# Threshold attention and mixer: weights transposed SBUF to SBUF, value product turned over, mixer in small pieces

## The chip, the cores and the metric

The kernel runs on one core of a Trainium2 chip. The metric is the device time of one execution in microseconds. Inputs and output lie in DRAM as float32.

## What is computed

Eight batches, eight heads, 576 positions, head size 64. Attention keeps only scores within tau = 0.02 of each row's maximum; the heads, laid side by side, form x (576 x 512), which goes through a mixer: a low-rank product over positions (rank 32), then a two-layer network over channels (512 to 2048 to 512), both with a residual.

```python
scores = scale * np.matmul(q, k.transpose(0, 1, 3, 2))
thresh = np.max(scores, axis=-1, keepdims=True) - tau
scores = np.where(scores >= thresh, scores, -1000000000.0)
attn = np.exp(scores - np.max(scores, axis=-1, keepdims=True))
attn = attn / (np.sum(attn, axis=-1, keepdims=True) + 1e-09)
x = np.matmul(attn, v)          # then the heads side by side: (B, 576, 512)
u = x + (x.transpose(0, 2, 1) @ U @ V).transpose(0, 2, 1)
out = u + np.maximum(u @ w_ch1, 0.0) @ w_ch2
```

## The kernel before

Work goes by pairs of heads: 32 pairs, four to a batch. For each pair:

- **Loads** (L104, L105, L111, L114, on POOL's queue): q and k in tiles of 96 rows, v in tiles of 128.
- **Transposes** (L132, L135, on PE): 12 transposes of 96 rows give q and k with both heads' 64 features on 128 partitions; ACT copies them out of PSUM and scales q by 1/8.
- **Scores** (L152): five row tiles (four of 128 rows, one of 64), per head a float32 product with 64 contracted rows, in two column halves of 288. A float32 matmul stands as two records in the trace, so a pair has 5 x 2 x 2 x 2 = 40. A score tile takes two PSUM banks; two such buffers exist.
- **Row work**, per head and row tile: DVE copies the scores out and takes the row maximum in one pass (L155), then the negated maximum (L166) and the threshold (L168); ACT takes the exponential (L171); DVE masks it, `(s >= thr) * e`, in bfloat16 (L178). That last step is put off by one tile (`deferred`).
- **Weights transposed**: SP writes each masked tile to a scratch in DRAM (L181), whose rows are padded from 576 to 640 columns by a fill (L306, on POOL); after a head's last tile, one transposing DMA (L184) brings all 576 rows back as `wt_sb`, keys on the partitions.
- **Value product** (L202), issued two pairs later: v is split into a bfloat16 part and a bfloat16 remainder with a column of ones between (L116 to L123), and for each of five row tiles and five key tiles the transposed weights are the stationary side and the 130 columns of v move: 50 matmuls a pair. ACT copies the result (L210), DVE adds the two parts (L211) and the ones column gives the denominator.

After a batch's fourth pair the mixer is queued as four stages, one run in each of the next pairs' turns: `mixer_m1` (division L218 to L223, cast L230, low-rank products L233 and L239), `mixer_m2` (transposes L253), `mixer_m3` (first layer, 128 matmuls L266, relu on ACT L273), `mixer_m4` (second layer, 80 matmuls L282, residual L285, output DMA). The last batch's stages run alone at the end. A scheduler puts the instructions of each engine in order; every engine then runs its own list in that order.

Of the kernel before, what the change touches and what calls it, by code (L numbers as in the profile page):

```python
# [12 lines left out]
ALU = mybir.AluOpType  # L13

# [4 lines left out]
NB96 = S // 96  # L19
QTILES = [(0, 128), (128, 128), (256, 128), (384, 128), (512, 64)]  # L20
KTILES = QTILES
SCHUNK = 288
WSCR_COLS = 640

DEBUG_X = False
# [3 lines left out]
def kernel(  # L29
# [16 lines left out]
    consts = ctx.enter_context(tc.tile_pool(name="consts", bufs=1))  # L46
    ident_f = consts.tile([P, P], FP32, name="ident_f")
    make_identity(nc, ident_f)
    zpad = consts.tile([96, NB96, WSCR_COLS - S], BF16, name="zpad")
    nc.vector.memset(zpad, 0.0)  # L50

    wpool = ctx.enter_context(tc.tile_pool(name="weights", bufs=1))
    W1b = wpool.tile([P, 4, F], BF16, name="W1b")
    W2b = wpool.tile([P, 16, DM], BF16, name="W2b")
    Ub = wpool.tile([P, 5, R], BF16, name="Ub")
    Vb = wpool.tile([R, S], BF16, name="Vb")

    xpool = ctx.enter_context(tc.tile_pool(name="xpool", bufs=2))

    rawpool = ctx.enter_context(tc.tile_pool(name="raw", bufs=2))  # L60
    vrawpool = ctx.enter_context(tc.tile_pool(name="vraw", bufs=4))
    vaugpool = ctx.enter_context(tc.tile_pool(name="vaug", bufs=4))
    qkTpool = ctx.enter_context(tc.tile_pool(name="qkT", bufs=4))
    sbpool = ctx.enter_context(tc.tile_pool(name="ssb", bufs=3))
    smallpool = ctx.enter_context(tc.tile_pool(name="small", bufs=24))
    avpool = ctx.enter_context(tc.tile_pool(name="avpool", bufs=4))
    epool = ctx.enter_context(tc.tile_pool(name="epool", bufs=3))
    wrowpool = ctx.enter_context(tc.tile_pool(name="wrows", bufs=6))
    wtpool = ctx.enter_context(tc.tile_pool(name="wtpool", bufs=4))
    mpool = ctx.enter_context(tc.tile_pool(name="mix", bufs=2))  # L70
    m1pool = ctx.enter_context(tc.tile_pool(name="mix1", bufs=1))
    opool = ctx.enter_context(tc.tile_pool(name="opool", bufs=3))
    dpool = ctx.enter_context(tc.tile_pool(name="wscr", bufs=8, space=bass.MemoryType.DRAM))
    psc = ctx.enter_context(tc.tile_pool(name="psc", bufs=2, space=bass.MemoryType.PSUM))
    pav = ctx.enter_context(tc.tile_pool(name="pav", bufs=2, space=bass.MemoryType.PSUM))
    psm = ctx.enter_context(tc.tile_pool(name="psm", bufs=2, space=bass.MemoryType.PSUM))

    with tc.tile_pool(name="wstage", bufs=2) as st:
        su = st.tile([P, 5, R], FP32, name="us_", tag="us_")
        nc.gpsimd.dma_start(su[:, 0:4, :], moe_U[0:4 * P, :].rearrange("(t p) r -> p t r", p=P))  # L80
        nc.gpsimd.dma_start(su[0:64, 4, :], moe_U[4 * P:S, :])
        nc.vector.tensor_copy(out=Ub[:, 0:4, :], in_=su[:, 0:4, :])
        nc.vector.tensor_copy(out=Ub[0:64, 4, :], in_=su[0:64, 4, :])
        sv = st.tile([R, S], FP32, name="vs_", tag="vs_")
        nc.gpsimd.dma_start(sv, moe_V[:, :])
        nc.vector.tensor_copy(out=Vb, in_=sv)
        for t in range(4):
            for qt in range(4):
                s1 = st.tile([P, F // 4], FP32, name="w1s", tag="stage_big")
                nc.gpsimd.dma_start(  # L90
                    s1, moe_w_ch1[t * P:(t + 1) * P, qt * (F // 4):(qt + 1) * (F // 4)]
                )
                nc.vector.tensor_copy(out=W1b[:, t, qt * (F // 4):(qt + 1) * (F // 4)],
                                      in_=s1)
        for c in range(16):
            s2 = st.tile([P, DM], FP32, name="w2s", tag="stage_big")
            nc.gpsimd.dma_start(s2, moe_w_ch2[c * P:(c + 1) * P, :])
            nc.vector.tensor_copy(out=W2b[:, c, :], in_=s2)

    def emit_raw_qk(b, hp):  # L100
        qpair = rawpool.tile([96, NB96, 2, D], FP32, name="qpair", tag="qpair")
        kpair = rawpool.tile([96, NB96, 2, D], FP32, name="kpair", tag="kpair")
        for j, h in enumerate((2 * hp, 2 * hp + 1)):
            nc.gpsimd.dma_start(qpair[:, :, j, :], q[b, h].rearrange("(t p) d -> p t d", p=96))  # L104
            nc.gpsimd.dma_start(kpair[:, :, j, :], k[b, h].rearrange("(t p) d -> p t d", p=96))  # L105
        return qpair, kpair

    def emit_v_build(b, hp):
        vraw = vrawpool.tile([P, 5, 2, D], FP32, name="vraw", tag="vraw")
        for j, h in enumerate((2 * hp, 2 * hp + 1)):  # L110
            nc.gpsimd.dma_start(  # L111
                vraw[:, 0:4, j, :], v[b, h][0:4 * P, :].rearrange("(t p) d -> p t d", p=P)
            )
            nc.gpsimd.dma_start(vraw[0:64, 4, j, :], v[b, h][4 * P:S, :])  # L114
# [30 lines left out]
    def emit_scores_and_w(b, hp, qTpk, kTpk, wscrs, strips_out, deferred):  # L145
        for i, (qs, nq) in enumerate(QTILES):
            for j in (0, 1):
# [40 lines left out]
                if deferred:  # L188
                    deferred.pop(0)()
# [137 lines left out]
    if n_pairs > 1:  # L327
        raw_tiles[1] = emit_raw_qk(*pairs[1])
# [82 lines left out]
```

## Time and profile before

| | us |
|---|---|
| median of 3 runs | 1102.98 |
| lowest and highest run | 1101.51, 1124.68 |
| span of the profiled execution, first to last instruction | 1099.2 |
| PE busy (matmuls) | 999.8 |
| DVE busy | 718.9 |
| ACT busy | 484.5 |
| POOL busy | 245.7 |

The profiled execution's own time is known by its span; the median of the runs lies 3.8 us above it. The page has one row for each group of like instructions: line, engine, operation, tiles written and read, count, then busy time and mean length, then the idle time of the engine ahead of them and what ended it. Busy time of a group counts overlapping instructions once, so on PE, where matmuls overlap, busy time over count is less than the mean length.

### The profile page before, as it was taken

The page shows a single profiled execution, that of the slowest core. Times are in us where ns is not written, and L with a number is a line of the kernel's source. Part 1 is how long each engine was busy: PE and PEld are TensorE (multiplying, and loading weights), DVE is VectorE, ACT ScalarE, POOL GpSimd, SP SyncE. Part 2 cuts the span into 40 slices and gives each one's busy share as a digit, 9 for nine tenths or more (in the row PEclk, how much of TensorE's full clock was granted, in tenths as well). Part 3 has the DMA queues.
Part 4 walks back from the last instruction along what each step waited for, and adds up shares of the span by engine and source line. Part 5 has one row for each costly group of instructions (what it writes and reads, how often), then busy time and mean ns, then how long its engine had stood idle before and what let it go on. Part 6 is the DMA issues. An engine that isn't in the chain of part 4 may idle for free.

```text
span 1099.2 us, 16099 instructions
## 1 busy us (share of the span) xinstructions
PE 999.8 (91%) x5168; PEld 558.7 (51%) x5168; DVE 718.9 (65%) x2396; ACT 484.5 (44%) x1089; POOL 245.7 (22%) x363
## 2 busy tenths in 40 slices
PE   4886877999999998999998998999999999999898
PEld 3443443565545654555544655555545555456444
DVE  4864676866768558766677568675587666785521
ACT  2332341573436633554325634456335644366141
POOL 6544576412112220312112211122203011000000
PEclk9999965899959997889958998699968999599969
DMA  5789787575335563565546663366534543343401
GB/s 168 210 227 164 173 186 149 137 160 140 114 93 155 135 153 98 115 139 118 148 102 134 116 163 100 95 138 138 152 97 128 132 116 114 84 119 92 114 0 44
DMA packets 252725, 141.73 MB, mean 129 GB/s; under 512 B 197808, under 2 KB 238784, under 8 KB 252640
## 3 DMA queue, kind: packets, MB, share of 16 engines
q1 hardware_dynamic: 233600, 99.12, 38.6%
q0 software_dynamic: 19040, 41.59, 14.7%
q8 instruction: 40, 0.66, 0.3%
q14 instruction: 45, 0.37, 0.1%
HBM read 36.85 MB, written 56.62 MB: 85 GB/s over the span
## 4 chain that ended last, share of the span: by engine, by line
PE 75%; DMA 12%; DVE 7%; issue 4%; ACT 2%; SPq 0%; POOL 0%; DVEq 0%; POOLq 0%; ACTq 0%
PE sc L152 24%; PE avps L202 14%; PE p1ps L266 13%; PE chps L282 13%; DMA wt_sb<-wscr 10%; PE qkTps L132 4%; PE utps L253 3%; PE ttps L233 2%; PE hps L239 2%; DVE s_sb L155 2%; DVE xun L223 2%; DMA wscr<-w_sb 1%; DVE w_sb L178 1%; PE qkTps L135 1%; SPq L184 0%
## 5 line engine op out<-in xcount | busy, mean ns | idle before, releaser
L152 PE MATMUL sc<-qkTpk 64*128 64x288 f32 (+1 forms) x1280 | 393.3, 514 | 16.9 <-DVE s_sb L155 16.4
L155 DVE TENSOR_SCALAR_CACHE_REDUCE s_sb<-sc 128x576 f32<-128x576 f32 (+1 forms) x320 | 237.9, 748 | 157.4 <-PE sc L152 155.9
L171 ACT ACTIVATE e_sb<-s_sb,negm 128x576 bf16<-128x576 f32 (+1 forms) x320 | 246.3, 775 | 176.8 <-DVE thr L168 99.4
L178 DVE SCALAR_TENSOR_TENSOR w_sb<-s_sb,thr,e_sb 128x576 bf16<-128x576 f32 (+1 forms) x320 | 258.9, 809 | 22.4 <-ACT e_sb L171 21.7
L152 PEld LDWEIGHTS sc<-qkTpk 64*128 64x128 f32 (+1 forms) x1280 | 207.5, 212 | 106.4 <-DVE s_sb L155 39.0
L202 PE MATMUL avps<-vaug,wt_sb 128*128 128x130 bf16 (+3 forms) x1600 | 212.9, 250 | 42.5 <-DMA wt_sb<-wscr 35.4
L202 PEld LDWEIGHTS <-wt_sb 128*128 128x128 bf16 (+3 forms) x1600 | 125.5, 107 | 201.2 <-issue 107.1
L266 PE MATMUL p1ps<-uT,W1b 128*128 128x288 bf16 x1024 | 157.0, 292 | 0.7
L210 ACT COPY avsb<-avps 128x130 f32<-128x130 f32 (+1 forms) x320 | 79.3, 266 | 167.0 <-PE avps L202 154.9
L282 PE MATMUL chps<-W2b,Rb 128*128 128x512 bf16 (+1 forms) x640 | 146.5, 380 | 0.0
L104 POOL DMA_DIRECT2D qpair<-in_q_dram x64 | 47.4, 741 | 394.0 <-PE qkTps L135 334.7
L273 ACT ACTIVATE Rb<-p1ps 128x288 bf16<-128x288 f32 x256 | 104.4, 410 | 58.4 <-PE p1ps L266 50.8
L266 PEld LDWEIGHTS <-W1b 128*128 128x128 bf16 x1024 | 95.8, 99 | 55.1 <-issue 29.6
L285 DVE TENSOR_TENSOR o_sb<-chps,u_f 128x512 f32<-128x512 f32 (+1 forms) x40 | 27.5, 688 | 105.9 <-PE chps L282 105.9
L282 PEld LDWEIGHTS <-Rb 128*128 128x128 bf16 (+1 forms) x640 | 60.6, 100 | 69.4 <-issue 3.6
L111 POOL DMA_DIRECT2D vraw<-in_v_dram x64 | 49.4, 771 | 199.5 <-DVE xun L211 101.9
L137 ACT ACTIVATE qkTpk<-qkTps 128x480 f32<-128x480 f32 x32 | 18.2, 570 | 132.3 <-PE qkTps L132 127.6
L211 DVE TENSOR_TENSOR xun<-avsb 128x65 f32<-128x65 f32 (+1 forms) x320 | 59.1, 216 | 24.2 <-ACT avsb L210 22.2
L105 POOL DMA_DIRECT2D kpair<-in_k_dram x64 | 47.6, 744 | 41.1 <-PE qkTps L135 37.8
L306 POOL DMA_DIRECT2D wscr<-zpad x64 | 46.8, 738 | 5.7 <-DMA vraw<-in_v_dram 4.0
L166 DVE TENSOR_SCALAR negm<-mrow 128x1 f32<-128x1 f32 (+1 forms) x320 | 46.2, 144 | 0.5
L168 DVE TENSOR_SCALAR thr<-mrow 128x1 f32<-128x1 f32 (+1 forms) x320 | 44.9, 140 | 0.0
(52 smaller groups left out, 525.3 us busy)
## 6 DMA issues: line engine op xcount, KB each, us to landing
wscr<-w_sb SPq DMA_DIRECT2D x256, 144.0 KB, 1.8
qpair<-in_q_dram POOLq DMA_DIRECT2D x64, 144.0 KB, 3.1
kpair<-in_k_dram POOLq DMA_DIRECT2D x64, 144.0 KB, 3.1
vraw<-in_v_dram POOLq DMA_DIRECT2D x64, 128.0 KB, 4.4
out_dram<-o_sb SPq DMA_DIRECT2D x32, 256.0 KB, 2.3
wscr<-zpad POOLq DMA_DIRECT2D x64, 72.0 KB, 4.7
wscr<-w_sb SPq DMA_DIRECT2D x64, 72.0 KB, 2.0
w1s<-in_moe_w_ch_dram POOLq DMA_DIRECT2D x16, 256.0 KB, 3.4
```

The costliest lines, as they stand in the source:

```text
L105: nc.gpsimd.dma_start(kpair[:, :, j, :], k[b, h].rearrange("(t p) d -> p t d", p=96))
L111: nc.gpsimd.dma_start(vraw[:, 0:4, j, :], v[b, h][0:4 * P, :].rearrange("(t p) d -> p t d", p=P))
L152: nc.tensor.matmul(sct[0:nq, ci, 0:SCHUNK], lq, rk, start=True, stop=True)
L155: nc.vector.tensor_scalar(out=s_sb[0:nq, :].rearrange("p (a c) -> p a c", a=2), in0=sct[0:nq, :, 0:SCHUNK], scalar1=0.0, scalar2=None, op0 ...
L171: nc.scalar.activation(out=e_sb[0:nq, :], in_=s_sb[0:nq, :], func=ACT.Exp, bias=negm[0:nq, :])
L178: nc.vector.scalar_tensor_tensor(out=w_sb[0:nq, :], in0=s_sb[0:nq, :], scalar=thr[0:nq, :], in1=e_sb[0:nq, :], op0=ALU.is_ge, op1=ALU.mult)
L202: nc.tensor.matmul(avps[0:nq, slot, :], wt_sb[0:nk, kt, qs:qs + nq], vaug[0:nk, kt, j, :], start=(kt == 0), stop=(kt == 4),)
L210: nc.scalar.copy(out=avsb[0:nq, :], in_=avps[0:nq, slot, :])
L211: nc.vector.tensor_add(out=xun[0:nq, qc, h, :], in0=avsb[0:nq, 0:D + 1], in1=avsb[0:nq, D + 1:2 * D + 2])
L266: nc.tensor.matmul(p1[:, 0:SCHUNK], W1b[:, dt_, ft * P:(ft + 1) * P], uT[:, dt_, ci * SCHUNK:(ci + 1) * SCHUNK], start=(dt_ == 0), stop=(d ...
L273: nc.scalar.activation(out=Rb[:, ft, ci * SCHUNK:(ci + 1) * SCHUNK], in_=p1[:, 0:SCHUNK], func=ACT.Relu)
L282: nc.tensor.matmul(chps[0:ns, :], Rb[:, ft, ss:ss + ns], W2b[:, ft, :], start=(ft == 0), stop=(ft == 15))
```

## The change

Nearly the whole body is written anew. What is computed stays; these parts differ:

- **Rows are renumbered.** Position p * 9 + t sits on partition p of tile t, so that a load takes runs of up to five rows; tile t holds nine 64-row pieces, two to a 128-row tile, the fifth tile having one. q, k and v take four loads each. U, V and the output follow the same numbering.
- **Transposes of q and k**: four of 128 rows and one of 64, each.
- **Scores**: both heads of a row tile get their buffers together and are issued in turn, column half by column half; the two 64-row tails share one buffer, one head on partitions 0 to 63, the other on 64 to 127. This gives nine row tiles a pair instead of ten. q is scaled by -1/8, so minimum takes the place of maximum and the negated maximum is not needed; one threshold instruction serves both heads.
- **Masking** (`scalar_tensor_tensor`) writes into a ring of eight tiles whose columns 576 to 639 are zero from the start, and also sums its rows, which gives the denominator.
- **Weights transposed** straight from that ring into `wT`, SBUF to SBUF, one DMA for each row tile and head (two for the shared tail), all from SP. The DRAM scratch, its writes and its fills are gone. One small DMA moves the 64 denominators of the tail's second head.
- **Value product turned over**: v (split in two parts as before, the cast on ACT, the remainder on POOL) is stationary, 64 columns for each head in its own half of the array's columns, and 288 columns of `wT` move: 5 x 2 x 2 x 2 = 40 matmuls a pair. The result is transposed back by five PE transposes, and the division is folded into the copy out of PSUM.
- **Mixer** cut into 84 pieces in a queue; after each row tile's scores two pieces of the value product of the pair before and five mixer pieces are issued. It starts after the next batch's first pair.
- **PSUM**: two score buffers (two banks each) as before; everything else shares four one-bank buffers instead of two and two.
- Large weights are cast by their DMA instead of on DVE.

The diff, cut to its core:

```diff
-                sct = psc.tile([P, 2, 512], FP32, name="sc", tag="sc")
-                lq = qTpk[64 * j:64 * j + 64, qs:qs + nq]
-                for ci in range(2):
-                    rk = kTpk[64 * j:64 * j + 64, ci * SCHUNK:(ci + 1) * SCHUNK]
-                    nc.tensor.matmul(sct[0:nq, ci, 0:SCHUNK], lq, rk, start=True, stop=True)
...
-                    nc.sync.dma_start(wscrs[j][qs:qs + nq, 0:S], w_sb[0:nq, :])
-                    if last_row:
-                        strips = wtpool.tile([P, 5, S], BF16, name="wt_sb", tag="wt_sb")
-                        nc.sync.dma_start_transpose(strips[:, :, :],
-                                                    wscrs[j][0:S, 0:WSCR_COLS])
...
+    psS = pool("psS", 2, PSUM)
+    ps1 = pool("ps1", 4, PSUM)
...
+                sct = [psS.tile([P, 2, 512], FP32, name="sc", tag="sc") for _ in range(2)]
+                for c in range(2):
+                    for j in range(2):
+                        hs = slice(64 * j, 64 * j + 64)
+                        nc.tensor.matmul(sct[j][:, c, 0:HC], self.qT[hs, i * P:(i + 1) * P],
+                                         self.kT[hs, c * HC:(c + 1) * HC], start=True, stop=True)
...
+                w_sb = w_ring[ring[0] % NW]
+                ring[0] += 1
+                nc.vector.scalar_tensor_tensor(
+                    out=w_sb[:, 0:S], in0=ssb[x], scalar=thr[:, x:x + 1], in1=esb[x],
+                    op0=ALU.is_le, op1=ALU.mult, accum_out=self.den[:, i, x:x + 1])
+                if i < 4:
+                    nc.sync.dma_start_transpose(self.wT[:, :, x, i * P:(i + 1) * P], w_sb[:, :])
+                else:
+                    for j in range(2):
+                        nc.sync.dma_start_transpose(self.wT[:, :, j, 512:S],
+                                                    w_sb[64 * j:64 * j + 64, :])
+            if i == 4:
+
+                nc.sync.dma_start(self.den[0:HB, 4, 1:2], self.den[HB:P, 4, 0:1])
...
+                for part in range(2):
+                    for c in range(2):
+                        for j in range(2):
+                            nc.tensor.matmul(
+                                st["av"][c][64 * j:64 * j + 64, 0:HC],
+                                self.vh[0:nk, kt, part, j, :],
+                                self.wT[0:nk, kt, j, c * HC:(c + 1) * HC],
+                                start=(kt == 0 and part == 0), stop=(kt == 4 and part == 1))
...
+        for i in range(NT):
+            pair.scores(i)
+            if i == 1 and p + 1 < NP:
+                pairs[p + 1].prepare_qk()
+            if i == 3 and p + 1 < NP:
+                pairs[p + 1].prepare_v()
+            pop(applyq, 2)
+
+            pop(mixq, 5)
+            if i == 1 and p >= 1:
+
+                applyq.extend(pairs[p - 1].apply_units(xs[pairs[p - 1].b]))
```

How the order of instructions moves, at three places.

On PE, in the middle of a pair before. Names are line, operation, tile written <- tiles read, shape; numbers tell buffers apart:

```order
L152 MATMUL sc_5634<-qkTpk_5065,qkTpk_5054 128x288 x2
L152 MATMUL sc_5649<-qkTpk_5065,qkTpk_5054 128x288 x2
L202 LDWEIGHTS wt_sb_5232
L202 MATMUL avps_5730<-vaug_4585,wt_sb_5232 128x130
...
L282 MATMUL chps_5816<-W2b_69,Rb_5338 128x512
...
L152 MATMUL sc_5664<-qkTpk_5065,qkTpk_5054 128x288 x2
```

and now:

```order
L174 MATMUL sc_3949<-qkT_3564,qkT_3554 128x288
L174 MATMUL sc_3950<-qkT_3564,qkT_3554 128x288
...
L322 MATMUL p1_3919<-uT_3522,W1b_66 128x288
...
L174 MATMUL sc_3949<-qkT_3564,qkT_3554 128x288
L174 MATMUL sc_3950<-qkT_3564,qkT_3554 128x288
...
L229 MATMUL av_3970<-wT_3470,vh_3408 64x288
L229 MATMUL av_3970<-wT_3470,vh_3408 64x288
```

The two heads now alternate; here the scheduler has also put five mixer pieces (20 matmuls) between the two column halves of one score group.

On DVE, one row tile before:

```order
L155 TENSOR_SCALAR s_sb_5160,mrow_5161<-sc_5157 128x576
L178 SCALAR_TENSOR_TENSOR w_sb_5154<-s_sb_5145,thr_5149,e_sb_5152 128x576
L166 TENSOR_SCALAR negm_5163<-mrow_5161 128x1
L168 TENSOR_SCALAR thr_5164<-mrow_5161 128x1
L155 TENSOR_SCALAR s_sb_5175,mrow_5176<-sc_5172 128x576
```

and now:

```order
L190 TENSOR_SCALAR s_sb_4254,m_4252<-sc_4246 128x576
L190 TENSOR_SCALAR s_sb_4256,m_4252<-sc_4247 128x576
L200 TENSOR_SCALAR thr_4253<-m_4252 128x2
L205 SCALAR_TENSOR_TENSOR w_ring3_73,den_4130<-s_sb_4254,thr_4253,e_sb_4258 128x576
L205 SCALAR_TENSOR_TENSOR w_ring4_74,den_4130<-s_sb_4256,thr_4253,e_sb_4260 128x576
```

Both reductions of a row tile now stand ahead of both maskings, with one threshold between.

On SP, about one pair before:

```order
L181 DMA wscr<-w_sb 128x576 x6
L181 DMA wscr<-w_sb 64x576
L184 DMA_TRANSPOSE wt_sb<-wscr 128x5x576
L181 DMA wscr<-w_sb 64x576
L181 DMA wscr<-w_sb 128x576
L184 DMA_TRANSPOSE wt_sb<-wscr 128x5x576
```

and now:

```order
L209 DMA_TRANSPOSE wT<-w_ring_75 128x5x128
L209 DMA_TRANSPOSE wT<-w_ring_76 128x5x128
L342 DMA out_dram<-o 64x512
L344 DMA out_dram<-o 64x512
L212 DMA_TRANSPOSE wT<-w_ring_77 128x5x64 x2
L216 DMA den<-den 64x1
```

Many small transposes stand where ten writes and two transposes stood, and the output's DMAs stand between them.

More of the change, by code (lines that the diff above doesn't have):

```diff
@@ L18, with rows @@
 R = 32
[L19 to L25, printed above, removed]
+HC = S // 2
+HB = 64
+NT = 5
+NPAIR = H // 2
+def rows(i):
+    return P if i < 4 else HB
 @with_exitstack
@@ L69 @@
[L69 to L81, printed above, removed]
+    NW = 8
+    w_ring = [wpool.tile([P, 640], BF16, name=f"w_ring{n}") for n in range(NW)]
+    for t_ in w_ring:
+        nc.gpsimd.memset(t_[:, S:640], 0.0)
@@ L95 @@
[L95 to L106, printed above, removed]
```

505 lines of the change are left out of this document (243 added, 262 removed).

## The prediction

> **What bounds the kernel now.** I read the page's totals first, then the chain that ended last, then time by windows, to see whether the totals hold in each stage.
>
> ```profile
> span 1099.2 us, 16099 instructions
> ...
> PE 999.8 (91%) x5168; PEld 558.7 (51%) x5168; DVE 718.9 (65%) x2396; ACT 484.5 (44%) x1089; POOL 245.7 (22%) x363
> ...
> PE 75%; DMA 12%; DVE 7%; issue 4%; ACT 2%; SPq 0%; POOL 0%; DVEq 0%; POOLq 0%; ACTq 0%
> ```
>
> PE is busy in 91% of the span and makes up 75% of the chain; no other engine passes 65%. So time comes out mainly where PE gets shorter. The windows show one batch (four pairs) in the steady state, then its two kinds of stage.
>
> ```profile
> 587.00:716.00 129.00, 121.59 (x646) 67.99 (x645) 87.87 (x295) 60.09 (x136) 21.76 (x33) 0.85 0.54 124
> ```
> ```profile
> 676.00:707.00 31.00, 28.86 (x106) 14.99 (x105) 22.89 (x75) 9.35 (x23) 2.91 (x4) 0.51 0.39 96
> ...
> 731.00:803.00 72.00, 70.23 (x426) 40.04 (x423) 47.51 (x161) 36.81 (x82) 13.68 (x20) 1.00 0.56 137
> ```
> ```profile
> core 0: 1099.2 us, clock 0.879
> ```
>
> Columns are the stretch, its length, busy time of PE, weight loads, DVE, ACT and POOL, then the granted clock, DMA share and GB/s. PE is busy 121.6 of 129 us. In the 31 us around the mixer's start (low-rank products and transposes) the clock is 0.51 and PE does 106 matmuls; in the 72 us with the dense mixer matmuls it is 1.00 and PE does 426. The mean over the run is 0.879. Thus a PE price read at full clock is divided by 0.879 below.
>
> **The change part by part.** First PE. The rows are: two groups with their busy time, then pieces of the timeline (start, length, count).
>
> ```profile
> L152 PE MATMUL sc<-qkTpk 64*128 64x288 f32 (+1 forms) x1280 | 393.3, 514 | 16.9 <-DVE s_sb L155 16.4
> ...
> L202 PE MATMUL avps<-vaug,wt_sb 128*128 128x130 bf16 (+3 forms) x1600 | 212.9, 250 | 42.5 <-DMA wt_sb<-wscr 35.4
> ```
> ```profile
> 500.12 0.63 PE L132 MATMUL qkTps<-ident_f,kpair 96*128 96x96 f32 x5
> ...
> 502.37 1.23 PE L152 MATMUL sc<-qkTpk 64*128 64x288 f32 x4 [0.37 <-DVE s_sb L155]
> ...
> 504.31 1.50 PE L152 MATMUL sc<-qkTpk 64*128 64x288 f32 x8
> ...
> 505.74 0.88 PE L202 MATMUL avps<-vaug,wt_sb 128*128 128x130 bf16 x7
> ```
> ```profile
> 1037.15 2.71 PE L202 MATMUL avps<-vaug,wt_sb 128*64 128x130 bf16 x25 [0.36 <-ACT avsb L210]
> ...
> 1057.40 20.39 PE L266 MATMUL p1ps<-uT,W1b 128*128 128x288 bf16 x128
> ```
>
> *Scores.* A pair has 40 records (1280/32) and costs 393.3/32 = 12.3 us of PE. One head of a row tile alone takes 1.23 us for four records; both heads together take 1.50 us for eight, and the next matmul starts 1.43 us after the first. The heads use different 64 rows of the array and run side by side, but only when both score buffers are free. The changed order always issues both heads column half by column half, and puts the two short tiles into one: five groups of 1.43 us, 7.15 us at full clock, 8.1 us at 0.879. That saves 4.2 us a pair. Bounds: 0 (the average of before stays) and 5.2 (full clock).
>
> *Value product.* 50 matmuls a pair become 40, now with 288 moving columns, the two heads in different column halves. Before: 212.9/32 = 6.7 us. No row shows two column halves at once. Nearest rows: 2.71/25 = 0.108 us for a 130-column one, 20.39/128 = 0.159 us for a 288-column one after another, half of that (0.08) if halves overlap fully. I take 0.11, near the middle: 4.4 us, 5.0 at 0.879, a saving of 1.7 (0.3 to 3.1).
>
> *Transposes.* q and k: 12 of 96 columns at 0.63/5 = 0.126 become ten of up to 128, the same within 0.2 us. New are five back-transposes of the result: 5 x 0.126 x 128/96 = 0.84, so +0.8 us with rounding, at 0.879 up to +1.0. The mixer's own matmuls are the same in number and shape, so nothing there.
>
> Next the path from the weights to the value product, on SP.
>
> ```profile
> L184 SPq DMA_TRANSPOSE wt_sb<-wscr x64: 2864/3350/5748, 49.3 to 1025.7; - x64
> ```
> ```profile
> wscr<-w_sb SPq DMA_DIRECT2D x256, 144.0 KB, 1.8
> ...
> wt_sb<-wscr SPq DMA_TRANSPOSE x64, 5.9
> ```
>
> The write to DRAM (1.8 us to landing) and the transpose behind it (5.9 us) come after the last row tile, and the value product waited 35.4 us in all for it (the L202 row). Now each row tile is transposed as soon as it exists and the product starts two row tiles of the next pair later. I take the 35.4 us, 1.1 a pair, as gone (0 to 1.1). On SP a transpose of 576 rows held the queue for 3.35 us; by rows, 128 of them take 0.74 us, so a pair's ten pieces (eight of 128, two of 64) take 6.7 us, far below a pair's time. Behind them on SP stand only the small denominator copy, 64 numbers, and the output's writes; a late one delays the next pair's product, nothing nearer. The 64 fills of the scratch's padding leave POOL, whose loads become twelve a pair.
>
> Then DVE and ACT, which must stay covered by PE.
>
> ```profile
> L178 DVE SCALAR_TENSOR_TENSOR w_sb<-s_sb,thr,e_sb 128x576 bf16<-128x576 f32 x256 | 207.5, 811 | 17.7 <-ACT e_sb L171 17.0
> L171 ACT ACTIVATE e_sb<-s_sb,negm 128x576 bf16<-128x576 f32 x256 | 197.0, 775 | 155.0 <-DVE thr L168 78.4 <-DVE negm L166 72.5
> L155 DVE TENSOR_SCALAR_CACHE_REDUCE s_sb<-sc 128x576 f32<-128x576 f32 x256 | 190.9, 749 | 150.7 <-PE sc L152 149.2
> ...
> L168 DVE TENSOR_SCALAR thr<-mrow 128x1 f32<-128x1 f32 x256 | 36.4, 142 | 0.0
> ...
> L223 DVE TENSOR_TENSOR xun<-xun,rec 128x512 f32<-128x512 f32 x32 | 21.9, 688 | 0.0
> ...
> L155 DVE DVE_READ_ACCUMULATOR s_sb<-sc 128x1 f32 x256 | 20.5, 80 | 0.0
> ```
>
> Nine tiles a pair in place of ten: reductions 9 x (0.749 + 0.080) = 7.5 us; weights 9 x (0.811 + 0.080, since the sum is now read out too) = 8.0; thresholds 5 x 0.142 = 0.7; the scaled copy out of PSUM 0.69 + about 0.3; reciprocals four at about 0.15. That is 17.8 us; the mixer adds 11 x 0.688 a batch, 1.9 a pair. DVE: 19.7 us a pair, 630 in all (718.9 before). ACT takes the v casts and the evacuation of the product but loses 320 small copies: near 475 us. Both lie under PE's new (999.8 - 32 x 5.1) / 32 = 26 us a pair; if that cover went, DVE's 630 would be the floor.
>
> *New coupling.* All PSUM users but the scores share four buffers; the product holds two for half a pair, which leaves two, as before, for the hidden layer. At some places the order puts 20 mixer matmuls (20 x 0.159 = 3.2 us) between the first and second column half of a score group, and the reduction waits that long. PE works meanwhile, so it costs only where DVE is late next. Bounds 0 and 3.2; I take 0.5 a pair.
>
> **Sum** per pair: -4.2 - 1.7 + 0.8 - 1.1 + 0.5 = -5.7 us; 32 x 5.7 = 182. The span goes from 1099.2 to 917. The median of the runs, 1102.98, is 3.8 above the profiled span, so about 920 us.
>
> **The rivals.**
>
> *Clock stays full.* The half-clock stretches sit where the mixer starts in one lump; now it is cut into pieces between scores. If they vanish, PE's new 837 us shrink by 0.121, 101 us: 820. For it: 1.00 in the dense 72 us. Against: the score-only pairs and the first batch remain, and in the 31 us row the clock was 0.51 with PE busy 28.9. Chance 0.12.
>
> The Trainium skill, "TensorE: Matmul & The Clock Gate", Part 1, says the clock halves after an idle window of about 3.4 us; by that rule the new order, with no such gap, would give this rival's 820. The trace disagrees: idle in the 31 us row is 2.1 us in all, and the clock was half; so the rule does not raise the chance.
>
> *PE and DVE take turns.* If DVE waits for the whole score group at each of 160 row tiles (1.43/0.879 = 1.63 us), it takes 630 + 260, and the head and tail come on top:
>
> ```profile
> 16.73 2.43 PE L152 MATMUL sc<-qkTpk 64*128 64x288 f32 x8 [0.49 <-ACT qkTpk L140]
> ```
> ```profile
> 1035.24 1.58 PEld L202 LDWEIGHTS <-wt_sb 128*128 128x128 bf16 x16 [0.41 <-issue]
> ```
>
> 17 us to the first score and 64 (1035.2 to 1099.2) at the end: 971, 975 with the rest. For it: the 149.2 us that the reduction already waited for scores. Against: two score buffers let PE run ahead. Chance 0.17.
>
> *Halves do not overlap.* Scores stay at 12.3 us and the product falls by 0.3 only: 917 + 134 + 45 = 1096, 1100. The 1.50 us row speaks against. Chance 0.06.
>
> *SP becomes the bound (slower).* No row has a transpose that reads SBUF. If its price goes by the instruction and not by the rows, ten times 3.35 us is 33.5 a pair: 32 x 33.5 + 17 + 64 = 1153, 1157 us. It decides from (917 - 81)/320 = 2.6 us a piece. For it: even the shortest of the 64 took 2.86. Against: all 64 had one size, so no row says that small ones cost as much. Chance 0.09.
>
> **How the numbers follow.** The forecast has 0.56; alone, with product and coupling at their lower bounds it gives 917 - 32 x 1.9 = 856, with product and DMA wait at their upper ones 917 + 32 x 2.5 = 997. With the rivals the range of 8 in 10 is 820 to 1045: it holds the forecast, turns, and half of the full clock, and leaves out no overlap and the SP bound. A measurement of this kernel can tell about 2% from no change. Faster by more: 0.56 + 0.12 + 0.17 = 0.85; within: 0.06; slower: 0.09.
>
> **What would show it.** Right: PE still the busiest engine near 840 us; score records in groups of eight within 1.5 us at full clock, their busy time near 260 us; value product near 160; DVE near 630; SP transposes under 1 us. Wrong: a transposing DMA above 2.6 us, product matmuls waiting for it, or DVE idle mostly for scores while PE idles too.

## The result, and the profile after

The changed kernel takes 877.97 us, the median of 4 runs (872.43 to 879.43). The kernel before, on the same chip, takes 1105.58 us (median of 4). The ratio is 0.794, with a 95% interval of 0.790 to 0.798. The profiled execution has a span of 877.7 us against 1099.2: 221.5 us came off.

First the head of the profile's page of the changed kernel, then its cores.

```profile
span 877.7 us, 14636 instructions
...
PE 793.2 (90%) x4914; PEld 456.0 (52%) x4944; DVE 557.7 (64%) x1597; ACT 431.6 (49%) x881; POOL 307.7 (35%) x473
```
```profile
core 0: 877.7 us, clock 0.894
```

PE is still the engine that is busy nearly all the time, and its busy time fell from 999.8 to 793.2 us, by 206.6. Its idle time fell from 99.4 (1099.2 - 999.8) to 84.5, by 14.9. So the gain is almost wholly in how long PE's work takes, and this is where the terms have to be found. PE's groups of the changed kernel (line, names, shapes, count, busy time, mean ns, idle time ahead and what ended it):

```profile
L174 PE MATMUL sc<-qkT 64*128 64x288 f32 x1024 | 242.8, 489 | 35.0 <-DVE s_sb L190 34.3 <-ACT qkT L139 0.4
L337 PE MATMUL ch<-W2b,Rb 128*128 128x512 bf16 (+1 forms) x610 | 146.2, 380 | 2.8 <-issue 1.4
L322 PE MATMUL p<-uT,W1b 128*128 128x288 bf16 x1024 | 142.6, 286 | 7.5 <-ACT Rb L325 7.1 <-ACT uT L305 0.2
L229 PE MATMUL av<-wT,vh 128*64 128x288 bf16 (+1 forms) x1280 | 130.2, 307 | 6.0 <-DMA wT<-w_ring 6.0
L182 PE MATMUL sc<-qkT 64*64 64x288 f32 x256 | 39.0, 424 | 2.9 <-DVE s_sb L190 1.9
...
L251 PE MATMUL xps<-ident,xT 128*128 128x128 f32 (+1 forms) x160 | 24.8, 284 | 0.4 <-ACT xT L238 0.4
```

The scores went from 393.3 us to 242.8 + 39.0 = 281.8, the value product from 212.9 to 130.2, the back transposes are new with 24.8, and the wait of the product for its weights is 6.0 us where it was 35.4. A stretch of the timeline at full clock shows how:

```profile
607.94 1.24 PE L174 MATMUL sc<-qkT 64*128 64x288 f32 x8
609.12 1.17 PE L229 MATMUL av<-wT,vh 128*64 128x288 bf16 x16
610.22 2.33 PE L337 MATMUL ch<-W2b,Rb 128*128 128x512 bf16 x10
612.48 1.24 PE L174 MATMUL sc<-qkT 64*128 64x288 f32 x8
613.65 1.17 PE L229 MATMUL av<-wT,vh 128*64 128x288 bf16 x16
```

A row tile's scores of both heads, eight records, take 1.24 us. Sixteen product matmuls take 1.17 us; with 0.29 us for the last one (the 286 ns of the L322 row, also 288 columns), that is (1.17 - 0.29) / 15 = 0.059 us each.

One batch in the steady state, cut at the pairs' first scores (start and end, length, busy PE, weight loads, DVE, ACT, POOL, then granted clock, DMA share and GB/s):

```profile
516.60:533.10 16.50, 15.48 (x114) 8.89 (x114) 14.08 (x39) 7.01 (x13) 9.06 (x14) 1.00 0.81 151
533.10:572.30 39.20, 37.69 (x178) 20.79 (x177) 22.60 (x64) 20.47 (x42) 9.31 (x14) 0.70 0.42 72
572.30:597.90 25.60, 24.43 (x183) 15.20 (x183) 15.77 (x47) 17.01 (x40) 9.54 (x15) 1.00 0.51 94
597.90:620.90 23.00, 21.88 (x146) 11.45 (x147) 17.56 (x50) 9.05 (x17) 9.45 (x15) 1.00 0.67 133
```

The four pairs are very uneven. The first has only the last nine pieces (18 matmuls) of the mixer that began three pairs earlier, and takes 16.5 us. The second, in which the mixer of the batch before starts, takes 39.2 us for 178 matmuls, at a clock of 0.70. This pair, not the sum of the work, is the place where the changed kernel still loses time.

### The profile page after: what moved, and what is told of

Same layout as the page of the kernel before. It is cut to its first block, busy times and chain, and to the rows that moved or that the text cites. A ratio compares the mean times of both kernels' runs of the same rounds, so it can differ in the third digit from the quotient of the medians.

```text
span 877.7 us, 14636 instructions
## 1 busy us (share of the span) xinstructions
PE 793.2 (90%) x4914; PEld 456.0 (52%) x4944; DVE 557.7 (64%) x1597; ACT 431.6 (49%) x881; POOL 307.7 (35%) x473
## 5 line engine op out<-in xcount | busy, mean ns | idle before, releaser
L197 ACT ACTIVATE e_sb<-s_sb,m 128x576 bf16<-128x576 f32 x288 | 215.4, 774 | 255.8 <-DVE s_sb L190 252.5
L190 DVE TENSOR_SCALAR_CACHE_REDUCE s_sb<-sc 128x576 f32<-128x576 f32 x288 | 209.0, 752 | 171.8 <-PE sc L174 122.0
L174 PE MATMUL sc<-qkT 64*128 64x288 f32 x1024 | 242.8, 489 | 35.0 <-DVE s_sb L190 34.3
L205 DVE SCALAR_TENSOR_TENSOR w_ring<-s_sb,thr,e_sb 128x576 bf16<-128x576 f32 x288 | 228.3, 819 | 64.8 <-ACT e_sb L197 51.6
L174 PEld LDWEIGHTS sc<-qkT 64*128 64x128 f32 x1024 | 128.8, 212 | 116.2 <-DVE s_sb L190 52.2
L322 PE MATMUL p<-uT,W1b 128*128 128x288 bf16 x1024 | 142.6, 286 | 7.5 <-ACT Rb L325 7.1
L337 PE MATMUL ch<-W2b,Rb 128*128 128x512 bf16 (+1 forms) x610 | 146.2, 380 | 2.8 <-issue 1.4
L229 PE MATMUL av<-wT,vh 128*64 128x288 bf16 (+1 forms) x1280 | 130.2, 307 | 6.0 <-DMA wT<-w_ring 6.0
L322 PEld LDWEIGHTS <-W1b 128*128 128x128 bf16 x1024 | 95.2, 97 | 51.2 <-issue 29.6
L325 ACT ACTIVATE Rb<-p 128x288 bf16<-128x288 f32 x256 | 99.9, 413 | 30.0 <-PE p L322 21.9
L90 POOL DMA_DIRECT2D kraw<-in_k_dram x64 | 43.6, 681 | 8.1 <-DMA W2b<-in_moe_w_ch_dram 6.5
L238 ACT COPY xT<-av 128x288 f32<-128x288 f32 x64 | 22.6, 401 | 46.7 <-PE av L229 46.0
L91 POOL DMA_DIRECT2D kraw<-in_k_dram x64 | 40.5, 632 | 5.1 <-DMA W2b<-in_moe_w_ch_dram 5.1
```

Source lines behind the costliest of these rows:

```text
L90: nc.gpsimd.dma_start(raw[0:HB, :, j, :], sv[:, 0:NT, j, :])
L91: nc.gpsimd.dma_start(raw[HB:P, 0:4, j, :], sv[:, NT:9, j, :])
L174: nc.tensor.matmul(sct[j][:, c, 0:HC], self.qT[hs, i * P:(i + 1) * P], self.kT[hs, c * HC:(c + 1) * HC], start=True, stop=True)
L190: nc.vector.tensor_scalar(out=s_sb.rearrange("p (a c) -> p a c", a=2), in0=sct[x][:, :, 0:HC], scalar1=0.0, scalar2=None, op0=ALU.add, op1 ...
L197: nc.scalar.activation(out=e_sb, in_=ssb[x], func=ACT.Exp, bias=m[:, x:x + 1], scale=-1.0)
L205: nc.vector.scalar_tensor_tensor(out=w_sb[:, 0:S], in0=ssb[x], scalar=thr[:, x:x + 1], in1=esb[x], op0=ALU.is_le, op1=ALU.mult, accum_out= ...
```

## The experiments

All ratios are to the kernel before, with their 95% intervals; the changed kernel has 0.794 (0.790 to 0.798). Where two intervals do not overlap, the two kernels differ. The kernel before was timed again in each series, with medians from 1105.58 to 1119.32 us, so differences in us between runs of different series are good to about 1%; in the series of `e5`, `e11`, `e12` and `e13` it ranged from 1100.69 to 1131.83 us, and those intervals are wider.

### What made the scores shorter

The prediction put it down to the two heads that stand side by side, column half by column half. The first try was to give the kernel before just that order of the source (`e1`):

```diff
-            for j in (0, 1):
-                sct = psc.tile([P, 2, 512], FP32, name="sc", tag="sc")
...
+            scts = [psc.tile([P, 2, 512], FP32, name="sc", tag="sc") for _ in range(2)]
+            for ci in range(2):
+                for j in (0, 1):
+                    nc.tensor.matmul(scts[j][0:nq, ci, 0:SCHUNK],
...
```

> The kernel before, with one change: a row tile's two score buffers are taken together, and the matmuls go column half by column half through both heads. Everything else stays. Theory (the scores got shorter because the two heads always run side by side): the score matmuls' busy time falls from 393 us to between 260 and 300, and with PE as the bound the run falls by 95 to 130 us, to 975 to 1010. Rival (the order alone brings little, because the reduction of a row tile now waits for both heads, or because the saving came with the shared buffers and pieces of the rest): busy time of the scores falls, but PE idle time grows by as much, and the run stays within 25 us of 1105.

Measured: 1111.07 us, ratio 0.998 (0.992 to 1.004), nothing. The order of the compiled program says why. Of the 128 row tiles with 128 rows, so many have their four score matmuls next to each other on PE's queue:

```
kernel before                      30
heads in turn in the source (e1)   43
changed kernel                     83
head by head in the source (e11)   91
other work between heads (e13)     11
mixer in four lumps (e3)           70
```

In the kernel before, the program's scheduler puts other matmuls into most row tiles, and the new order in the source makes only 13 more of them whole. Standing together did not suffice there either: in the traces, none of the 30 whole groups of the kernel before and one of the 43 of `e1` takes less than 1.35 us from its first start to its last end, against 61 of the 83 in the changed kernel. A likely reason, which no run isolates, is that the reductions of the two heads stay apart there, so that the second score buffer comes free later than the first. The run hardly tested the theory (the expectation below says that its groups were cut as often as before; it is 85 of 128 against 98). The next one tests it from the other side, by pulling the heads of the changed kernel apart (`e13`; `between` issues one piece of the product and three of the mixer):

```diff
-                for c in range(2):
-                    for j in range(2):
+                for j in range(2):
+                    if j == 1:
+                        between()
+                    for c in range(2):
```

> The changed kernel, with other work put between the two heads of a row tile: head 0's score matmuls, then one piece of the product and three of the mixer, then head 1's matmuls, then the rest as before. Same work, same buffers, both reductions still together. The run with only the order of the emission changed in the kernel before brought nothing, but there the groups of both heads were as often cut apart as in the kernel before itself, so that it did not test the side-by-side running. Theory (the shorter scores come from heads that stand next to each other): a group of eight records in 1.24 us becomes two of four in 0.75 to 1.23 us each; 128 groups x 0.5 to 1.2 us at a mean clock of 0.89 is 70 to 170 us more, so 950 to 1050. Rival (side by side brings little; the shorter scores came from the clock and the buffers): 870 to 900.

Measured: 946.31 us, ratio 0.849 (0.834 to 0.864), 68 us more than the changed kernel. Its group of the scores and a piece of its timeline:

```profile
L176 PE MATMUL sc<-qkT 64*128 64x288 f32 x1024 | 329.9, 460 | 26.9 <-DVE s_sb L192 26.0 <-DMA sv<-in_moe_V_dram 0.4 <-ACT qkT L139 0.4
```
```profile
643.62 1.23 PE L176 MATMUL sc<-qkT 64*128 64x288 f32 x4
644.79 0.68 PE L231 MATMUL av<-wT,vh 128*64 128x288 bf16 x8
645.63 0.81 PE L339 MATMUL ch<-W2b,Rb 128*128 128x512 bf16 x3 [0.16 <-issue]
646.37 1.23 PE L176 MATMUL sc<-qkT 64*128 64x288 f32 x4
```

One head alone takes 1.23 us, as long as both together (1.24). The scores' busy time went up by 87 us, from 242.8 to 329.9. The theory held, though 946 us lies just below the 950 that it gave as its lower end. The clock was 0.938 here, higher than the changed kernel's 0.894, so the clock is not what made the scores longer. Then the order inside a whole group (`e11`):

```diff
-                for c in range(2):
-                    for j in range(2):
+                for j in range(2):
+                    for c in range(2):
```

> The changed kernel, with the four score matmuls of a row tile issued head by head in place of column half by column half; the groups stay whole. Theory (next to each other in the order of the kernel before, eight records take 1.50 us, alternating 1.24): 0.26 us x 160 groups at a clock of 0.89 is 45 us of PE, so 905 to 925. Rival (once they stand next to each other the order within does not matter): 870 to 890.

Measured: 877.08 us, ratio 0.793 (0.781 to 0.804), no difference that can be told. The group is as short head by head:

```profile
588.29 1.25 PE L174 MATMUL sc<-qkT 64*128 64x288 f32 x8
592.32 1.25 PE L174 MATMUL sc<-qkT 64*128 64x288 f32 x8
```

The rival was right. What counts is that the four matmuls stand together, not how they alternate.

### The value product in column halves

`e2` runs the product of the changed kernel one head after the other, so that neighbours go to the same 64 columns:

```diff
-                        for j in range(2):
-                            nc.tensor.matmul(
...
+            steps = [(j, kt) for j in range(2) for kt in range(NT)]
...
+                for j, kt in steps[2 * u:2 * u + 2]:
```

> The changed kernel, with the value product one head after the other: same 1280 matmuls, but neighbours now go to the same 64 columns. Theory (the two column halves overlap fully: 0.059 us each in a run of 16 against about 0.12 alone): 1280 x 0.06 = 77 us more at full clock, 86 at a mean clock of 0.89, and PE is the bound, so 940 to 965 against 878. Rival (the product is bound by its weight loads or by a rate that does not depend on the order): within 15 us of 878, and a run of 16 still in about 1.2 us.

Measured: 903.31 us, ratio 0.815 (0.808 to 0.822): 25 us more, between the two forecasts. From its groups, its timeline and its cores:

```profile
L174 PE MATMUL sc<-qkT 64*128 64x288 f32 x1024 | 216.5, 452 | 30.1 <-DVE s_sb L190 29.7 <-ACT qkT L139 0.4
L231 PE MATMUL av<-wT,vh 128*64 128x288 bf16 (+1 forms) x1280 | 185.2, 290 | 0.5 <-DMA wT<-w_ring 0.3 <-ACT qkT L137 0.3
```
```profile
619.22 2.15 PE L231 MATMUL av<-wT,vh 128*64 128x288 bf16 x16
```
```profile
core 0: 899.2 us, clock 0.970
```

Sixteen take 2.15 us, (2.15 - 0.29) / 15 = 0.124 each, against 0.059: in the changed kernel the two column halves run fully side by side, here they do not, and the product costs 55 us more (185.2 - 130.2). But the granted clock rose from 0.894 to 0.970, and with it the scores of the full row tiles became 26 us shorter (242.8 to 216.5). PE's busy time as a whole rose by only 34.7 us (793.2 to 827.9), and its idle time fell by 13.2, so the span is 21.5 us longer. Of the 55 us that the side-by-side product saves, more than half is thus given back elsewhere, part of it by a lower clock.

### The way of the weights

`e9` gives the kernel before the direct transposes alone, `e4` takes them from the changed kernel, and `e6` issues each of them twice.

```diff
-                    nc.sync.dma_start(wscrs[j][qs:qs + nq, 0:S], w_sb[0:nq, :])
...
+                    nc.sync.dma_start_transpose(strips_out[j][:, :, qs:qs + nq], w_sb[0:nq, :])
```

> The kernel before, with only the way of the weights changed: each row tile of a head is transposed at once from SBUF to SBUF out of a ring of six zero-padded tiles; the scratch in DRAM, its fills and the two whole transposes of a pair are gone. Theory (what the way through DRAM costs there is the 35.4 us that the product waited): 1065 to 1100. Rival 1 (the wait only moves: the twenty-odd us of idle time come back for the scores' reductions): within 10 us of 1105. Rival 2 (the DRAM traffic slowed other things too): under 1060.

Measured: 1066.08 us, ratio 0.959 (0.953 to 0.965). Its span is 1064.8 us, 34.4 below the 1099.2 of before, and the product hardly waits for weights any more:

```profile
L204 PE MATMUL avps<-vaug,wt_sb 128*128 128x130 bf16 (+3 forms) x1600 | 207.8, 251 | 9.1 <-ACT avsb L212 5.6 <-DMA wt_sb<-w_ring 3.3
```

The theory held: 35.4 us of wait became 3.3, and nothing else came in its place, since PE's idle time fell by 36.3 us (99.4 to 63.1) and its busy time stayed (999.8 and 1001.7). The median lies 48 us below that of the kernel before in this series (1113.99); the profiles account for 34 of them.

```diff
-                    nc.sync.dma_start_transpose(self.wT[:, :, x, i * P:(i + 1) * P], w_sb[:, :])
+                    nc.sync.dma_start(self.scr[x][i * P:(i + 1) * P, :], w_sb[:, :])
...
+                    for j in range(2):
+                        nc.sync.dma_start_transpose(self.wT[:, :, j, :], self.scr[j][:, :])
```

> The changed kernel, with the weights going through DRAM again: each row tile is written to a scratch in DRAM (640 columns, padding from the ring, so no separate fills), and two whole transposes per pair come behind the last row tile. Theory (the direct transpose only took away a wait of about 1 us a pair, and the product now starts two row tiles into the next pair, which covers a write and a transpose of about 8 us): 878 to 915. Rival (the direct transpose carries a good part of the gain): the product waits for its weights in every pair, 3 us or more each, and the run takes over 960.

Measured: 954.75 us, ratio 0.860 (0.853 to 0.867), 77 us more; between the two, nearer the rival. Its group of the product:

```profile
L232 PE MATMUL av<-wT,vh 128*64 128x288 bf16 (+1 forms) x1280 | 156.9, 347 | 98.7 <-DMA wT<-wscr 98.5
```

It waits 98.5 us, 3 us in each pair. The write lands after 3.9 us (median); the two transposes stand behind one another on SP, which each holds for 3.5 us, and land after 8.0. By these numbers the second one is there some 15 us after the last write is issued, more than the two row tiles that the product starts late (an estimate of 10 us, from a pair's 26). With the shorter pairs the product waits nearly three times the 35.4 us of before.

```diff
                     nc.sync.dma_start_transpose(self.wT[:, :, x, i * P:(i + 1) * P], w_sb[:, :])
+                    nc.sync.dma_start_transpose(wD[:, :, x, i * P:(i + 1) * P], w_sb[:, :])
```

> The changed kernel, with each transposing transfer issued a second time, into a tile that nobody reads. Theory (a transpose holds SP for 1.22 us, so ten of them take 12.3 us of a pair's 26, and twice as many 24.6 us: still no bound, only later in the short pairs): 875 to 905. Rival (the transposing transfers are near a limit of their own behind SP, so twice as many double the time to landing and the product waits for its weights): over 920.

Measured: 1051.89 us, ratio 0.946 (0.940 to 0.952): 174 us more. The theory fell, and the rival's time (over 920) came without its mechanism: the transposes land in the same 2.7 us (median of the first ones), and the product's wait for them grew only from 6.0 to 31.5 us, yet the run is far longer. The timeline of SP and DVE's waits of this run:

```profile
568.02 2.34 SPq L210 DMA_TRANSPOSE wT<-w_ring  x1
570.40 1.27 SPq L211 DMA_TRANSPOSE wD<-w_ring  x1
571.77 1.20 SPq L214 DMA_TRANSPOSE wT<-w_ring  x1
...
576.92 0.59 SPq L220 DMA_DIRECT2D den<-den  x1
577.62 1.22 SPq L210 DMA_TRANSPOSE wT<-w_ring  x1
```
```profile
DVE rec L245 <- DMA den<-den: 167.4, 25, 22.1
```

SP is issuing one transfer right behind the other; its issues add up to 915 us of the 1050, where they are 484 of 878 in the changed kernel. The denominator's small copy stands last in its pair. It goes out late, though once issued it lands in 1.8 us (median), and DVE waits for it ahead of its reciprocals: 167.4 us in 25 waits, against 31.1 us in the changed kernel. The next score reductions stand behind the reciprocals in DVE's list and wait with them. PE's idle time grew by 119 us (84.5 to 203.7) and its busy time by 53, at a clock of 0.850. So SP has room for one set of transposes and not for two. No run gives the small copy a queue of its own, so that it carries the whole delay is argued from these waits.

### The mixer's pieces and the clock

`e3` ties the mixer's 84 pieces into four lumps, one at the start of a pair:

```diff
-        return units
+        return [lump(units[0:7]), lump(units[7:12]), lump(units[12:44]), lump(units[44:84])]
...
-            pop(mixq, 5)
+            pop(mixq, 1 if i == 0 else 0)
```

> The changed kernel, with the mixer's 84 pieces tied into four lumps (7, 5, 32 and 40 pieces), one at the start of each pair of the next batch. Theory A (the small pieces matter: between scores the mixer's matmuls run at fuller clock and cover the waits for DVE, which explains 31 us of mixer time and 15 us of idle time that came off in the change): 905 to 930, with p1, ch, tps, hps and ups together up by 20 to 40 us and more PE idle time. Theory B (the mixer's pieces bring nothing of their own; the four shared buffers and the shorter scores did it): within 12 us of 878.

Measured: 919.66 us, ratio 0.827 (0.818 to 0.835), 42 us more. The small pieces are worth that much, as theory A said, but not for its reason. In the profile (span 928.2 us) the mixer's five groups add up to 329.7 us, 28 less than the 357.9 of the changed kernel, and PE's idle time is 87.1 us against 84.5. What got longer is the scores:

```profile
L174 PE MATMUL sc<-qkT 64*128 64x288 f32 x1024 | 296.5, 504 | 49.7 <-DVE s_sb L190 49.1
```

With the 43.1 us of the short tiles that is 339.6 us against 281.8, and the product has 143.3 against 130.2. One part of how is in the table above, 70 whole score groups against 83; what the clock adds is not separated by this run.

The uneven pairs suggested the next two. `e12` pops three mixer pieces a row tile in the first mixed batch and four or five later, which holds back 24 pieces of a mixer's second matmul, and spreads them between the first twelve pieces of the next mixer. x gets a third buffer for that.

```diff
-            pop(mixq, 5)
+            if p <= 2 * NPAIR:
+                pop(mixq, 3)
+            else:
+                pop(mixq, 5 if i == 4 else 4)
...
-            mixq.extend(mixer_units(b - 1, xs[b - 1]))
+            mixq[:] = merge(mixq, mixer_units(b - 1, xs[b - 1]))
```

> The changed kernel, with the mixer's first twelve pieces (cast, low-rank products, transposes) spread between some 24 pieces of the second matmul of the batch before, which are held back for it (three mixer pieces a row tile in the first mixed batch, then four or five; a third buffer for x). Same work. Theory (the clock goes to half where PE has little work in a window of 3.4 us, which is where the mixer starts, and takes 14 to 24 us of work to come back; covered, it stays full): mean clock 0.95 or more, half of the 37.6 us in each 204.8 comes off, 19 x 4 = 75 us at most: 805 to 850. Rival (the clock follows a budget of work done and drops elsewhere): clock near 0.89 and 865 to 895.

Measured: 821.85 us, ratio 0.737 (0.725 to 0.750), 56 us below the changed kernel. Its cores, PE's line of the page, and a batch in windows as above:

```profile
core 0: 819.5 us, clock 0.973
```
```profile
PE 745.4 (91%) x4910; PEld 426.1 (52%) x4944; DVE 553.2 (68%) x1597; ACT 421.6 (51%) x881; POOL 306.7 (37%) x473
```
```profile
477.60:499.50 21.90, 21.69 (x153) 12.26 (x154) 16.60 (x49) 11.72 (x26) 10.13 (x15) 1.00 0.68 118
499.50:522.20 22.70, 20.78 (x128) 9.49 (x130) 19.50 (x55) 11.62 (x22) 8.86 (x15) 1.00 0.66 132
522.20:544.50 22.30, 21.98 (x160) 13.12 (x159) 16.93 (x50) 12.30 (x25) 8.92 (x14) 1.00 0.60 125
544.50:568.20 23.70, 22.69 (x182) 14.86 (x181) 15.92 (x47) 16.26 (x39) 9.29 (x14) 1.00 0.63 100
```

The four pairs are now even, the clock is 1.00 in all of them, and a batch takes 90.6 us in place of 104.3. PE's busy time fell by 47.8 us with the same matmuls. The time lies in the theory's 805 to 850. The control, `e15`, keeps the rates, the held-back pieces and the third buffer, but puts the 24 pieces ahead of the next mixer's start:

```diff
-        return res + old + new[12:]
+        return list(old) + new
```

> The control of the run with the covered start of the mixer: the same rates (three pieces a row tile in the first mixed batch, then four or five), the same third buffer for x and the same 24 pieces held back, but these now stand all ahead of the next mixer's first twelve pieces, and none between them. Theory (it is the dense work between the first pieces that keeps the clock up): the clock falls back to near 0.90 and the run to 855 to 885. Rival (the even rates, the third buffer or the later place of the start did it): within 12 us of 822.

Measured: 820.76 us, ratio 0.736 (0.728 to 0.744), clock 0.952. The theory fell: dense work *between* the mixer's first pieces is not needed. In the pair in which the mixer of a batch starts, the clock is 1.00 here too:

```profile
426.00:449.80 23.80, 23.07 (x156) 13.37 (x155) 19.23 (x56) 12.65 (x26) 9.18 (x14) 1.00 0.62 114
```

The two runs share the even rates, the 24 pieces (between or right ahead) and the third buffer; which of the three does it, no run separates.

### The head

In the changed kernel PE stands still for 19 us in the second pair. The timeline and DVE's wait:

```profile
60.21 2.28 PE L174 MATMUL sc<-qkT 64*128 64x288 f32 x6 [19.00 <-DVE s_sb L190]
```
```profile
DVE rec L241 <- DMA den<-den: 31.1, 6, 18.5
```

Again DVE waits for the small copy behind the transposes, and these landed up to 21.2 us after their issue (6.7 at most after the first 140 us) while the eight loads of 512 KB of the mixer's weights were under way (a DMA share of 1.02 in the first window below). `e5` issues these one at a time in pairs 1 to 4, and `e14` does the same on top of `e12`:

```diff
+            if 1 <= p <= 4 and i in (1, 3):
+                load_big(2 * (p - 1) + (i == 3))
             pair.scores(i)
```

> The changed kernel, with the eight large loads of the mixer's weights issued one at a time in pairs 1 to 4, not all ahead of pair 0. Theory (the stall of 19.0 us on PE at 41 to 60 us and the 44 us of the second pair come from transposes that landed up to 21 us late behind these loads): 850 to 862, and no transpose lands later than about 8 us. Rival (the head is bound by the first loads and the half clock there, not by the large ones): within 5 us of 878.

> The run with the covered start of the mixer, and the eight large weight loads issued one at a time in pairs 1 to 4 as well. Alone the late loads took 19 us of idle time from PE, but PE's busy time grew by 12 us, since more of the first batch ran at half clock. Theory (the same trade in the first batch): 812 to 822. Rival (with the clock full later on, the whole 19 us come off): 798 to 808.

Measured: `e5` 875.64 us, ratio 0.789 (0.781 to 0.796), not to be told from the changed kernel, as the rival had it; `e14` 814.30 us, 0.733 (0.727 to 0.739), inside its theory's range, but not to be told from `e12`. The stall did go, but the time did not follow: in `e5` PE's idle time fell by 18.8 us (84.5 to 65.7) and its busy time rose by 12.2. From the windows of the changed kernel, then of `e5`:

```profile
30.00:75.00 45.00, 19.32 (x101) 12.47 (x102) 17.70 (x57) 10.27 (x19) 19.62 (x30) 0.58 1.02 163
75.00:130.00 55.00, 46.76 (x288) 27.07 (x285) 45.80 (x143) 31.21 (x59) 35.78 (x54) 0.90 0.86 143
```
```profile
30.00:75.00 45.00, 35.62 (x207) 21.71 (x204) 35.45 (x113) 20.64 (x39) 30.77 (x48) 0.96 1.18 180
75.00:130.00 55.00, 46.14 (x210) 24.42 (x209) 36.91 (x111) 24.61 (x44) 22.74 (x32) 0.70 0.87 139
```

From 30 to 130 us the changed kernel does 389 matmuls and `e5` 417: in the first stretch `e5` is 106 ahead, in the second, at a clock of 0.70, it loses 78 of them. The theory's mechanism held in the main (the latest transpose landed after 12.9 us, not about 8) and its price did not.

## Why the prediction was right, step by step

It said 920 us, within 820 to 1045, and faster with 0.85; 878 came. The main forecast, PE's work shortened and PE still the bound, is what happened. That the total came within 5% is in part luck, since single sizes missed by more and partly cancel: the scores gave less than expected, the value product and the mixer more. Of the signs named beforehand, PE stayed the busiest engine (793.2 us, 840 named) and whole score groups took 1.24 us (within 1.5 named); a transpose under 1 us on SP did not come. By its terms, over 32 pairs:

- **Scores**, -134 us expected, -111.5 measured. The mechanism, the two heads side by side, was shown by `e13`. Half of the given reason was wrong: alternating the column halves does nothing (`e11`), and that both heads run together is decided by what the program's order puts between them, which the source's order of the scores does not settle (`e1`). A whole group at full clock is even shorter than the 1.43 us that were taken. But only 83 of 128 groups are whole and some fall into half clock, which is the likely reason why less than expected came off; no run parts the two.
- **Value product**, -54 expected, -82.7 measured. This was the most mis-sized term: 0.11 us a matmul at full clock was taken, near the middle of the bounds, and 0.059 came in whole runs of 16, the lower bound of 0.08 undercut. `e2` shows the overlap to be the cause.
- **Back transposes**, +26 expected, 24.8 measured. The q and k transposes, held equal, went from 71.9 us to 65.9.
- **The DMA wait**, -35.4 expected; -29.4 measured, as 6.0 us of it are left. `e9`, which changes this alone, keeps 3.3. `e4` shows that it was worth more in the new order, where keeping the old way would have cost 77 us.
- **The new coupling** of scores and mixer matmuls, +16 expected. PE's waits for a score buffer did grow by 21.0 us (16.9 to 35.0 + 2.9), but 19.0 of them are the one stall in the head, which comes from the small copy and not from mixer matmuls inside a score group.
- **The mixer**, taken as nothing, became 29 us shorter: its five groups have 387.1 us before (157.0 + 146.5 + 37.6 + 23.4 + 22.6) and 357.9 after. The matmuls are the same, so it is probably a matter of when they run; 30 of the second layer's 640 are missing from the trace, at 0.24 us each, so the fall may be up to 7 us smaller. Small pieces are not the cause: in `e3`, with lumps, these groups are shorter still (329.7). Why they became shorter stays open.
- **SP**: the step that was wrong is the price by rows. A transpose of 128 rows was put at 0.74 us and one of 64 at 0.37. The rows say otherwise:

```profile
L209 SPq DMA_TRANSPOSE wT<-w_ring x256: 1198/1222/8859, 17.9 to 820.5; - x128
...
L212 SPq DMA_TRANSPOSE wT<-w_ring x64: 1175/1244/2737, 47.4 to 824.4; - x64
```

  128 and 64 rows cost the same 1.2 us: the price goes by the instruction, as the rival on SP had it, only that it is 1.22 and not 3.35. Ten are 12.3 us of a pair's 26, so SP is no bound. The prediction put the point from which SP decides at 2.6 us a piece; `e6`, with 1.22 + 1.28 = 2.5, already ran 174 us longer, so the point lies lower. It also said of the small copy behind the transposes that a late one delays the next product and nothing nearer; `e6` and the head show that it holds DVE, and through it the scores.
- **DVE**, 630 expected, 557.7 measured; it stayed covered.
- **Clock**: the forecast divided by the mean of before, 0.879, and 0.894 came. The rival with the clock at full named 820 us, and it did not come about. That `e12` and `e15`, at clocks of 0.973 and 0.952, take 822 and 821 us is luck and does not confirm its price. It started from 837 us of PE work and took off 101; the changed kernel has 793.2, and by the same rule a full clock would leave 793.2 x 0.894 = 709, with the 84.5 us of idle time 794 us.

The sum -204.6 of the measured changes in PE's busy time (-111.5 - 82.7 + 24.8 - 6.0 - 29.2) stands against the 206.6 that PE's busy time lost; with the 14.9 us of idle time that makes the 221.5 us of the span.

## What to carry to other kernels

Where two matmuls use different rows or columns of the array, price them by whether they stand next to each other in the compiled order, count there how many do, and look in the trace whether one of them still waits for its buffer. When PE is the bound, look at its clock stage by stage: spreading the same work differently over the stages (with one more buffer) took 56 us off this kernel, more than several of the edits brought. Of a queue with room left, ask which small transfer stands last in it and which in-order engine waits for that one.

## What the runs showed of the hardware

- **The clock fell without a long idle gap.** Around the mixer's start of one batch in the changed kernel, PE's timeline and then windows:

```profile
534.69 1.23 PE L174 MATMUL sc<-qkT 64*128 64x288 f32 x6 [0.17 <-DVE s_sb L190]
537.04 0.90 PE L282 MATMUL tps<-xb,Ub 128*32 128x512 bf16 x2 [1.12 <-ACT xb L275]
```
```profile
535.10:538.50 3.40, 2.08 (x10) 0.79 (x6) 3.40 (x10) 2.72 (x7) 2.86 (x6) 1.00 0.43 85
538.50:562.40 23.90, 23.90 (x82) 12.72 (x81) 14.25 (x40) 9.67 (x19) 5.72 (x9) 0.50 0.53 88
562.40:565.80 3.40, 3.40 (x33) 1.93 (x29) 1.20 (x4) 1.95 (x5) 0.00 (x0) 1.00 0.21 42
```

  PE was busy 2.08 of 3.40 us, with no gap above 1.12, and the clock was at half for the next 23.9 us although PE was never idle in them. The Trainium skill, "TensorE: Matmul & The Clock Gate", section "HAM oscillation — how this bites in real kernels", has it that gaps above about 3.4 us throttle the clock. Here it fell with none above 1.12 us, and a busy PE was not enough to lift it again. Cut into stretches of 3.4 us, the half-clock time has 10, 8, 13, 10, 10, 15 and 26 matmuls (one across a border counts in both), and the clock is full right after the last of these; what exactly lifts it is open.
- **With the denser product the clock was lower**: 0.894 to 0.916 in the four runs with the column halves side by side, 0.960 to 0.987 in the four with the same matmuls one after the other (`e2`).
- **A transposing transfer from SBUF to SBUF** held SP for 1.22 us with 128 rows and 1.24 with 64, and landed after 2.7 us (median); behind large loads, up to 21.2 us.
